# Nine token tiles transposed by DMA, a searched start-up order and VectorE exp from step 6 in a one-core attention and FFN kernel

## The chip, the cores and the metric

The kernel runs on one core of one Trainium2 chip. The metric is the device time of one execution in microseconds (us). Times of a kernel are medians of its runs; where two kernels are compared in several rounds, they ran in turn on the same chip. Runs marked "one look" below are single executions and have no interval. The traces are of one execution each. In the record the time of one and the same kernel goes with the mean clock granted to TensorE in that execution: the kernel before took 773.5 to 773.9 us where that was 0.996, and 778.6 to 778.8 us where it was 0.987 to 0.989. Differences of 1 to 2 us between two single traces are to be read with that in mind.

Engines are named as in the profile: PE is TensorE (matmul), PEld its weight loads, DVE is VectorE, ACT is ScalarE, POOL is GpSimd, SP is SyncE, and SPq is the queue from which SP issues DMA transfers.

## The reference

With S = 2048 tokens, D = 640, 32 heads of 20, one shared key head and one shared value head, and F = 1728:

```python
x  = A_x                                   # 1 x 2048 x 640, bf16
xn = layernorm(x)
q  = xn @ wq                               # 32 heads of 20
k  = xn @ wk ; v = xn @ wv                 # one head of 20 each
o  = softmax(q k^T / sqrt(20)) v           # 2048 x 2048 per head
return x + o @ wo + silu(xn @ w1) @ w2
```

## The kernel before

A list scheduler in Python places every instruction on its engine ahead of time, with a cost model of its own. On the chip the orders are fixed; only semaphores decide when an instruction starts. The scheduler also places filler matmuls on zeros, whose results nobody uses, where it expects TensorE to wait.

The main loop has 688 *steps*: 43 groups of three heads (for 512 queries) times 16 key tiles. A step is three score matmuls of 512 columns, the exp of the three blocks, and the products P·V of an earlier step. ScalarE takes three blocks of a step, or two when VectorE takes the third by integer arithmetic on the bits (a "VectorE exp"). VectorE exps need a second copy of the keys with an offset, `kT1`, which POOL writes.

Before the loop can run freely comes the start-up ("prologue"): 16 token tiles are normalised, transposed, and turned into keys (`k` jobs), values (`v` jobs) and queries (`q` jobs). `PRO` is the order of these jobs. They are interleaved with the first exp steps.

```python
NBLK = 34                                  # ring of exp results, blocks of 512
PRO = "t4 t5 t6 k2 t7 t8 k3 t9 t10 k4 t11 t12 k5 t13 t14 v0 k6 t15 k7 q1 v1 v2 v3"
...
self.xn = self.w2[:, 0:4, :]               # four slots for normalised tiles
...
def want_dve(self, t):                     # may step t give a block to VectorE?
    if self.pro_left or t % KT >= KT - NOD:    # not while prologue jobs are left
        return False
    back = ...                             # VectorE's backlog in the model
    return back < DVE_TH
...
def tr_job(n):                             # transpose of tile n: five matmuls into PSUM,
    ...                                    # then one copy out by VectorE or ScalarE
...
def k_job(j):
    ...                                    # VectorE copies the keys out of PSUM, then POOL:
    sc.new("pool", t_pool(256), lambda g: g.tensor_scalar(d1, dst, self.offk[:, :], 1.0, ALU.add,
                                                          ALU.mult), [("kT", j), ("offk",)], [("kT1", j)], ...)
```

Heads 0 to 7 get their queries from two early jobs. Head 8 (step 32 is the first that uses it) gets them from a later job, `q0_0`, which makes those of heads 8 to 14: five matmuls, one copy to SBUF by VectorE, and seven small copies from SBUF to SBUF, all issued by SP. They share one semaphore, so whoever needs one of the seven waits for all.

```python
def qd_job(self, c, m, step=-1):           # q0_0 is c = 0, m = 0: columns 160 to 287 of wq
    ...
    sem = sc.sem(f"q{c}_{m}")
    for h in range(lo // DH, -(-hi // DH)):    # one copy per head: seven of them
        ...
        ops.append(sc.dma("sp", lambda q, ...: q.dma_start(
            self.qT[r:r + z - a, h // 4, c % 2, :], self.qd[a - lo:z - lo, sl, :]), [("qd", sl)], ...,
            sem=sem, name="qdma"))
    for op in ops:
        op.inc_no = len(ops)               # a reader waits for the count of all
```

The softmax here doesn't subtract the row's maximum and nothing guards it: scores larger than these inputs give would overflow.

## Time and profile before

| | before |
|---|---|
| time, first three runs | 776.55 us (776.13 to 778.77) |
| span in the profile | 775.3 us |
| first exp on ScalarE | 18.22 us |
| exp of step 21 / step 32 / last (687) | 59.30 / 71.95 / 753.34 us |
| ScalarE busy, 18.2 to 58.6 us | 31.62 of 40.40 us |
| ScalarE busy, 80 to 748.9 us | 658.84 of 668.90 us |

The prediction shows the lines these come from. "Exp of step n" is the start of the exp that comes n-th on ScalarE, counted from 0 in the trace; as every step has exactly one, the same n is the same work in every kernel here. The difference of two such starts is called the *lead* of one kernel.

### The profile page before, as it was taken

To read this page: it belongs to the slowest core of one execution; us is meant where nothing else is said; L and a number is where in the kernel's file an instruction comes from. 1 tells how busy PE (TensorE), PEld (TensorE's weight loads), DVE (VectorE), ACT (ScalarE), POOL (GpSimd) and SP (SyncE) were. 2 spreads that over 40 slices of the span, in tenths; PEclk is the share of its full clock that TensorE was granted. 3 is DMA by queue.
4 is the path that set the end of the run, shared out by engine and by line. 5 is a ranking of instruction groups with operands and counts; after the bars stand their busy time and mean duration, and the time that the engine had idled before them with its cause. 6 is when DMAs were issued, how large, how long until landed. Compare 5 with 4: busy or idle time off the path is not lost. (4 is left out here: it accounts for less than half of the span.)

```text
span 775.3 us, 17568 instructions
## 1 busy us (share of the span) xinstructions
PE 742.5 (96%) x6934; PEld 245.8 (32%) x6934; DVE 681.3 (88%) x1350; ACT 725.8 (94%) x772; POOL 26.2 (3%) x73
## 2 busy tenths in 40 slices
PE   8888998999999999999999999999999999999997
PEld 4432222222233333322223333322223333222334
DVE  7547999999999898999999999899999799899985
ACT  6879999999999999999999999999999999999960
POOL 4800000000000000000000000000000000000000
PEclk9989999999999999999999999999999999999999
DMA  9130000000110000000001000000010000000100
GB/s 283 56 115 8 10 10 8 10 8 8 42 35 23 19 10 26 25 8 2 2 1 35 26 25 23 14 17 5 2 35 18 19 19 18 2 1 1 29 1 35
DMA packets 27062, 20.05 MB, mean 26 GB/s; under 512 B 14790, under 2 KB 26342, under 8 KB 26982
## 3 DMA queue, kind: packets, MB, share of 16 engines
q1 hardware_dynamic: 25670, 18.89, 8.5%
q8 instruction: 56, 0.92, 0.5%
q10 hardware_dynamic: 1312, 0.05, 0.1%
q14 instruction: 24, 0.20, 0.1%
HBM read 11.36 MB, written 2.62 MB: 18 GB/s over the span
## 5 line engine op out<-in xcount | busy, mean ns | idle before, releaser
L748 ACT ACTIVATE sbt<-psall 128x1024 bf16<-128x1024 f32 (+2 forms) x688 | 697.5, 1162 | 18.9 <-PE psall L730 14.4
L762 DVE TENSOR_SCALAR sbt<-psall 128x512 int16<-128x512 f32 x560 | 375.7, 685 | 42.9 <-PE psall L730 36.4
L730 PE MATMUL psall<-sbt 32*128 32x512 bf16 x2048 | 269.6, 385 | 18.9 <-ACT sbt L748 11.7
L808 PE MATMUL psall<-sbt 128*32 128x512 bf16 x3329 | 258.1, 384 | 0.8 <-DVE sbt L1400 0.4
L820 DVE TENSOR_SCALAR sbt<-sbt 128x1536 int16<-128x1536 int16 (+2 forms) x420 | 204.0, 507 | 4.4 <-PE psall L808 2.0
L730 PEld LDWEIGHTS psall<-sbt 32*128 32x128 bf16 x2048 | 69.5, 91 | 257.0 <-ACT sbt L748 117.8
L808 PEld LDWEIGHTS psall<-sbt 128*32 128x32 bf16 x3329 | 70.3, 95 | 113.1 <-issue 64.2
L986 PE MATMUL psall<-sbt 128*128 128x512 bf16 (+1 forms) x280 | 87.7, 388 | 1.8 <-DVE sbt L999 1.6
L1047 PE MATMUL psall<-sbt 128*128 128x320 bf16 x448 | 87.0, 302 | 1.1 <-DVE sbt L961 1.0
L1047 PEld LDWEIGHTS psall<-sbt 128*128 128x128 bf16 x448 | 35.1, 97 | 44.1 <-issue 32.7
L999 DVE SCALAR_TENSOR_TENSOR sbt<-sbt,psall 128x512 bf16<-128x512 bf16 (+1 forms) x56 | 38.2, 681 | 4.4 <-ACT sbt L994 4.0
L994 ACT ACTIVATE sbt<-psall 128x512 bf16<-128x512 f32 (+1 forms) x56 | 39.7, 708 | 0.0
L882 DVE CAST sbt<-psall 128x512 bf16<-128x512 f32 (+1 forms) x43 | 29.5, 685 | 5.0 <-PE psall L808 4.9
L986 PEld LDWEIGHTS psall<-sbt 128*128 128x128 bf16 (+1 forms) x280 | 19.3, 98 | 40.9 <-issue 28.2
L1052 PE MATMUL psall<-sbt 128*128 128x320 bf16 x160 | 30.4, 302 | 0.7 <-DVE sbt L1030 0.7
L667 PE MATMUL psall<-sbt 128*128 128x512 bf16 (+4 forms) x103 | 28.5, 408 | 1.9 <-POOL sbt L1199 1.4
L954 PE MATMUL psall<-sbt 128*128 128x512 bf16 (+1 forms) x95 | 28.0, 384 | 0.0
L654 PE MATMUL psall<-sbt 128*32 128x512 bf16 (+8 forms) x85 | 25.1, 353 | 0.0
L1070 DVE SCALAR_TENSOR_TENSOR sbt<-psall,sbt 128x320 bf16<-128x320 f32 x32 | 15.0, 485 | 4.1 <-PE psall L1052 3.1
L917 DVE TENSOR_TENSOR sbt<-psall,sbt 128x240 bf16<-128x240 f32 (+2 forms) x46 | 17.2, 379 | 0.2
L1052 PEld LDWEIGHTS psall<-sbt 128*128 128x128 bf16 x160 | 12.6, 97 | 13.1 <-issue 7.0
L1352 DVE COPY sbt<-psall 128x640 bf16<-128x640 bf16 x14 | 6.7, 489 | 10.3 <-PE psall L1341 10.1
(79 smaller groups left out, 179.6 us busy)
## 6 DMA issues: line engine op xcount, KB each, us to landing
sbt<-in_A_x_dram SPq DMA_DIRECT2D x32, 160.0 KB, 3.3
out_dram<-sbt SPq DMA_DIRECT2D x16, 160.0 KB, 1.8
sbt<-in_B_w_dram SPq DMA_DIRECT2D x5, 432.0 KB, 6.4
sbt<-sbt SPq DMA_DIRECT2D x105, 20.0 KB
sbt<-in_B_w_dram SPq DMA_DIRECT2D x13, 160.0 KB, 3.4
sbt<-in_A_wo_dram SPq DMA_DIRECT2D x5, 160.0 KB, 6.5
sbt<-in_A_wq_dram SPq DMA_DIRECT2D x5, 140.0 KB, 3.6
sbt<-sbt SPq DMA_TRANSPOSE x16, 2.6
```

What stands on the lines that cost most here:

```text
L667: return pe.matmul(self.bk(b, 0, n), self.zero[:, 0:P], self.zero[:, 0:n], start=True, stop=True)
L730: ins = pe.matmul(self.bk(par3 + j), self.kT[r:r + SLOT, kk, kt * P:(kt + 1) * P], self.qT[r:r + SLOT, h // 4, (x // H) % 2, :], start=Tru ...
L748: return a.activation(self.E[:, b0 * QW:(b0 + na) * QW], self.ps[:, par3 * BANK:(par3 + na) * BANK], AF.Exp, scale=ACT_SCALE)
L762: return v.tensor_scalar(self.Z[:, zs, zp * QW:(zp + 1) * QW], self.bk(bb), 0.0, ZMAX, ALU.max, ALU.min)
L808: return pe.matmul(self.bk(UBANK, 0, QW, q * SLOT, (q + 1) * SLOT), self.v[:, w, kt, :], x, start=start, stop=stop, tile_position=(0, q * ...
L820: sc.new("dve", t_dve_4x(w), lambda v, k=k: v.tensor_scalar(self.Y[:, zs, k, 0:n * QW], Z, float(PH[k + 1][0]), None, ALU.add), zk, [("Y", ...
L882: return v.tensor_copy(self.U[0:rows, up, :], self.bk(UBANK, 0, QW, 0, rows))
L986: return pe.matmul(self.bk(b, 0, QW, 0, rows), self.w1[:, k, fk * P:fk * P + rows], self.xnT[:, k, c * QW:(c + 1) * QW], start=(k == 0), s ...
L994: sc.new("act", t_act(QW), lambda a: a.activation(t, src, AF.Tanh, scale=0.5), [("B", b)], [("tb", tp)], prio=X_PRIO, name=f"th{c}_{fk}")
L999: sc.new("dve", t_dve_ps(QW), lambda v: v.scalar_tensor_tensor(out=self.hT[0:rows, fk, :], in0=t, scalar=1.0, in1=src, op0=ALU.add, op1=AL ...
L1047: return pe.matmul(self.bk(b, 0, 320), self.hT[0:rows, fk, i * P:(i + 1) * P], self.w2[0:rows, fk, e0:e0 + 320], start=(m == 0), stop=(m = ...
L1052: return pe.matmul(self.bk(b, 0, 320), self.oT[:, k, i * P:(i + 1) * P], self.wo[:, k, e0:e0 + 320], start=(m == 0), stop=(m == tot - 1))
```

## The change

The intent is a shorter start-up. Three parts can be told apart:

1. **Transposes.** Tiles 4 to 7 and 11 to 15 are transposed by DMA from SP's queue, and every normalised tile has its own place (`xa(n)`), where before there were four slots.
2. **Order.** A new order of the jobs, another division of the layer norm's statistics, square roots and norms among the engines, found by a search.
3. **VectorE exp from step 6.** `want_dve` no longer waits until the start-up jobs are done.

```diff
-PRO = "t4 t5 t6 k2 t7 t8 k3 t9 t10 k4 t11 t12 k5 t13 t14 v0 k6 t15 k7 q1 v1 v2 v3"
-ACT_STATS = (3, 6, 9, 12)
-NW_ENG = ("dve", "pool", "pool")
-NORM_ENG = ("pool",) * 4 + ("pool", "act") * 4
-BATCHES = ((0, 4), (4, 10), (10, 16))
+DT = (4, 5, 6, 7, 11, 12, 13, 14, 15)
+DVE_FROM = 6
+PRO = "v0 t8 t9 k2 t10 k3 k4 k5 q1 v1 k6 k7 v2 v3"
+ACT_STATS = (2, 4, 6, 8, 9, 12)
+NW_ENG = ("dve", "pool", "pool", "dve")
+NORM_ENG = ("dve", "act", "dve", "dve", "pool", "pool", "dve", "act", "dve", "pool", "act", "act")
+BATCHES = ((0, 4), (4, 8), (8, 12), (12, 16))
...
     def want_dve(self, t):
-        if self.pro_left or t % KT >= KT - NOD:
+        if t < DVE_FROM or t % KT >= KT - NOD:
             return False
...
-        self.xn = self.w2[:, 0:4, :]
+        def xa(n):
+            if n < 13:
+                return self.w2[:, n if n < 4 else n + 1, :]
+            return oflat[:, (n - 13) * D:(n - 12) * D]
...
+        for n in range(4, NT):
+            norm(n, NORM_ENG[n - 4], NORM_P, self.batch[n])
+            if n not in DT:
+                continue
+            op = sc.dma("sp", lambda q, n=n: q.dma_start_transpose(
+                self.xnT[:, :, n * P:(n + 1) * P], xa(n)), xnk(n), [("xnT", n)], D * P * 2,
+                sem=sem(f"xT{n}"), name="xTd")
```

(Cut: the issue of the loads of w1 and wo moves behind the transposes, the blank fills of qT move ahead of them, and the scheduler's model of DMA times is adapted.)

More of the change, by code (lines that the diff above doesn't have):

```diff
@@ L63 @@
 Q_EVERY = 2
-PRO = "t4 t5 t6 k2 t7 t8 k3 t9 t10 k4 t11 t12 k5 t13 t14 v0 k6 t15 k7 q1 v1 v2 v3"
-ACT_STATS = (3, 6, 9, 12)
-NW_ENG = ("dve", "pool", "pool")
-NORM_ENG = ("pool",) * 4 + ("pool", "act") * 4
-BATCHES = ((0, 4), (4, 10), (10, 16))
+DT_ISSUE = 1.28
+DT = (4, 5, 6, 7, 11, 12, 13, 14, 15)
+NORM_P = 0.05
+DVE_FROM = 6
[4 more added lines that the diff above has]
+BATCHES = ((0, 4), (4, 8), (8, 12), (12, 16))
 class Op:
@@ L178, in commit @@
         if op.dma:
+            if op.name in ("oTd", "xTd"):
+                self.dma_t = op.end
             self.dma_t = max(getattr(self, "dma_t", 0.0), op.end) + op.mode / 230e3
-            op.avail = max(op.end + (2.6 if op.name == "oTd" else 2.0), self.dma_t + 1.6)
+            op.avail = op.end + 1.6 if op.name in ("oTd", "xTd") else max(op.end + 2.0, self.dma_t + 1.6)
         else:
@@ L1016, in try_oT @@
                 sem=self.s_oT[i], name="oTd")
+            op.dur = DT_ISSUE
             op.inc_no = len(self.oT_made)
@@ L1176, in prologue @@
                            for c in range(DC)], ("wqd", 1), P * D * 2)
-        load_w("sp", "1", [lambda q, c=c: q.dma_start(self.w1[:, c, :], self.B_w1[c * P:(c + 1) * P, :])
-                           for c in range(DC)], ("w1",), P * F * 2)
-        load_w("sp", "o", [lambda q, c=c: q.dma_start(self.wo[:, c, :], self.A_wo[c * P:(c + 1) * P, :])
-                           for c in range(DC)], ("wo",), P * D * 2)
         w2p = []
@@ L1187, in load_w2 @@
         def load_w2():
-            load_w("sp", "2", w2p, ("w2",), P * D * 2, [("xn", i) for i in range(4)] + [("idf",)])
+            load_w("sp", "2", w2p, ("w2",), P * D * 2, [("xn", i) for i in range(14)] + [("idf",)])
         np_ = sc.new
@@ L1232, in prologue @@
                 [("idf",)], [("stk",)])
-        for c in range(DC):
-            pool(0.7, lambda g, c=c: g.tensor_scalar(self.wo[:, c, :], self.wo[:, c, :], 2.0, 1.0, ALU.mult, ALU.mult),
-                 [("wo",)], [("wo",)])
         def wkrep(a):
@@ L1277, in mvk, with xnk @@
             return [("mv", n) for n in range(a, b_)]
+        oflat = self.o[:, :, :, :].rearrange("p a b c -> p (a b c)")
+        def xa(n):
+            if n < 13:
+                return self.w2[:, n if n < 4 else n + 1, :]
+            return oflat[:, (n - 13) * D:(n - 12) * D]
+        def xnk(n):
+            return [("xn", n)] + (self.okeys if n >= 13 else [])
         def norm(n, eng, prio, ra):
-            xs = n % 4
             if eng == "act":
                 np_("act", t_act(D) + 0.186, lambda v: v.activation(
-                    self.xn[:, xs, :], self.xslot(n), AF.Identity, scale=self.rstd[:, n:n + 1],
-                    bias=self.nb[:, n:n + 1]), self.xkeys(n) + [("nb", n), ("rs", ra)], [("xn", xs), ("xnv", n)],
+                    xa(n), self.xslot(n), AF.Identity, scale=self.rstd[:, n:n + 1],
+                    bias=self.nb[:, n:n + 1]), self.xkeys(n) + [("nb", n), ("rs", ra)], [("xn", n)],
                     prio=prio, name=f"norm{n}")
@@ L1287, in norm @@
             np_(eng, 0.36 if eng == "dve" else 0.87, lambda v: v.tensor_scalar(
-                self.xn[:, xs, :], self.xslot(n), self.rstd[:, n:n + 1], self.nb[:, n:n + 1], ALU.mult, ALU.add),
-                self.xkeys(n) + [("nb", n), ("rs", ra)], [("xn", xs), ("xnv", n)], prio=prio, name=f"norm{n}")
+                xa(n), self.xslot(n), self.rstd[:, n:n + 1], self.nb[:, n:n + 1], ALU.mult, ALU.add),
+                self.xkeys(n) + [("nb", n), ("rs", ra)], [("xn", n)], prio=prio, name=f"norm{n}")
         def newton(a, b_, pr, eng):
@@ L1335, in prologue @@
                     norm(n, "dve", 0.05, a)
+        for n in range(4, NT):
[5 more added lines that the diff above has]
+                sem=sem(f"xT{n}"), name="xTd")
+            op.dur = DT_ISSUE
+            op.inc_no = 1
+        load_w("sp", "1", [lambda q, c=c: q.dma_start(self.w1[:, c, :], self.B_w1[c * P:(c + 1) * P, :])
+                           for c in range(DC)], ("w1",), P * F * 2)
+        load_w("sp", "o", [lambda q, c=c: q.dma_start(self.wo[:, c, :], self.A_wo[c * P:(c + 1) * P, :])
+                           for c in range(DC)], ("wo",), P * D * 2)
+        for c in range(DC):
+            pool(0.7, lambda g, c=c: g.tensor_scalar(self.wo[:, c, :], self.wo[:, c, :], 2.0, 1.0, ALU.mult, ALU.mult),
+                 [("wo",)], [("wo",)])
+        for par in range(2):
+            for ht in range(2 if par == 0 else 0, HT):
+                np_("dve", 0.31, lambda v, par=par, ht=ht: v.tensor_scalar(
+                    self.qT[:, ht, par, :], self.zero[:, 0:QW], self.offq[:, :], None, ALU.add),
+                    [("zero",), ("offq",)], [("qb", par, h) for h in range(4 * ht, 4 * ht + 4)],
+                    prio=6.0 + par, name="qz")
         def tr_job(n):
-            xs = n % 4
             mms = []
@@ L1340, in f @@
                 def f(pe, b, k=k):
-                    return pe.transpose(self.bk16(b)[:, k * P:(k + 1) * P], self.xn[:, xs, k * P:(k + 1) * P],
+                    return pe.transpose(self.bk16(b)[:, k * P:(k + 1) * P], xa(n)[:, k * P:(k + 1) * P],
                                         self.idb[:, :])
@@ L1347, in consume @@
                 dst = self.xnT[:, :, n * P:(n + 1) * P]
-                if n in (0, 2) or (n >= 4 and not self.started):
+                if n in (0, 2):
                     sc.new("act", t_act(D), lambda a: a.activation(dst, src, AF.Copy), [("B", b)], [("xnT", n)],
@@ L1353, in consume @@
                            prio=0.5 if n < 4 else 3.0, name=f"xT{n}")
-                if n == NT - 1:
+                if n == max(i for i in range(13) if i not in DT):
                     load_w2()
-                    for par in range(2):
-                        for ht in range(2 if par == 0 else 0, HT):
-                            np_("dve", 0.25, lambda v, par=par, ht=ht: v.tensor_scalar(
-                                self.qT[:, ht, par, :], self.zero[:, 0:QW], self.offq[:, :], None, ALU.add),
-                                [("zero",), ("offq",)], [("qb", par, h) for h in range(4 * ht, 4 * ht + 4)],
-                                prio=6.0 + par, name="qz")
-                if n + 4 < NT:
-                    m = n + 4
-                    norm(m, NORM_ENG[m - 4], 0.5, self.batch[m])
-            return Job(f"tr{n}", mms, [("xnv", n), ("xn", xs), ("idb",)], consume)
+            return Job(f"tr{n}", mms, xnk(n)[:1] + [("idb",)], consume)
         def k_job(j):
```

## The prediction

> **What bounds the kernel now.** I read the engine totals first, then the busy time by stretch, then the timeline of ScalarE over the first 70 us, and last the waits of that stretch. The totals of the page:
> ```profile
> PE 742.5 (96%) x6934; PEld 245.8 (32%) x6934; DVE 681.3 (88%) x1350; ACT 725.8 (94%) x772; POOL 26.2 (3%) x73
> ...
> L748 ACT ACTIVATE sbt<-psall 128x1024 bf16<-128x1024 f32 (+2 forms) x688 | 697.5, 1162 | 18.9 <-PE psall L730 14.4
> L762 DVE TENSOR_SCALAR sbt<-psall 128x512 int16<-128x512 f32 x560 | 375.7, 685 | 42.9 <-PE psall L730 36.4
> ```
> TensorE's 96% contains filler matmuls, so it is no proof. The 688 exps of ScalarE (one per step: three 512-wide score blocks, or two when VectorE takes the third) fill 697.5 of 775.3 us. Whether that binds everywhere shows in the busy time by stretch (columns: window, its length, busy us of each engine with its count of instructions, granted TensorE clock, DMA share, GB/s):
> ```profile
> 0.00:18.20 18.20, 16.09 (x84) 7.54 (x84) 12.87 (x48) 10.73 (x23) 8.28 (x35) 1.00 0.89 274
> 18.20:58.60 40.40, 35.39 (x316) 15.22 (x314) 20.33 (x64) 31.62 (x26) 17.91 (x39) 0.92 0.29 95
> 58.60:80.00 21.40, 18.68 (x175) 5.94 (x178) 16.82 (x34) 20.13 (x21) 0.00 (x0) 1.00 0.03 7
> 80.00:748.90 668.90, 651.72 (x6215) 205.96 (x6207) 614.24 (x1167) 658.84 (x697) 0.00 (x0) 1.00 0.06 16
> 748.90:776.00 27.10, 20.64 (x160) 11.11 (x156) 17.02 (x39) 4.46 (x7) 0.00 (x0) 0.92 0.07 25
> ```
> From 80 to 748.9 us ScalarE is busy 658.84 of 668.90 us: that loop is bound by exp. In the start-up it is not: between the first exp (18.22 us) and 58.6 us ScalarE idles 40.40 - 31.62 = 8.8 us, and VectorE works only 20.33 of 40.40 us. ScalarE's timeline (start, us taken, operation, count, idle before) says where:
> ```profile
> 18.22 5.48 ACT L748 ACTIVATE sbt<-psall 128x1536 bf16<-128x1536 f32 x4 [0.81 <-PE psall L730]
> ...
> 27.91 0.92 ACT L1282 ACTIVATE sbt<-sbt 128x640 bf16<-128x640 bf16 x1 [2.99 <-PE psall L1341]
> 28.73 2.77 ACT L748 ACTIVATE sbt<-psall 128x1536 bf16<-128x1536 f32 x2
> ...
> 46.11 1.45 ACT L748 ACTIVATE sbt<-psall 128x1536 bf16<-128x1536 f32 x1 [1.08 <-PE psall L730]
> 51.31 16.90 ACT L748 ACTIVATE sbt<-psall 128x1536 bf16<-128x1536 f32 x15 [3.75 <-PE psall L808]
> ```
> Two big holes. At 24.9 us a norm needs the slot that the transpose of an earlier tile still holds (only four slots), and TensorE waits for the square root of tiles 4 to 9 on POOL. At 47.6 us the 34-block ring of exp results is full, and the products P·V that would free it wait for v jobs placed last in the order. All of the first 21 exps are three blocks wide; the first VectorE exp begins at 58.62 us, the first two-block one on ScalarE at 59.30 us.
>
> **What the Trainium skill says.** "Perfetto Trace Analysis", Optimization Strategy, says that a kernel can have several regimes, and to look for the gaps of the engine that should be full; that is the reading above, and the trace agrees (78% busy in the start-up, 98.5% in the loop). "DMA: Bandwidth & Descriptors", DMA Transpose, allows a transpose only from the SP or ACT queue, for 2-byte types, into SBUF; and two streams of them must not overlap. Here all come from SP, so one stream. The kernel before already has 16 of them: issue 1.23 us, landing 2.6 us in the median (2.4 to 4.1). "TensorE: Matmul & The Clock Gate", Part 4, says that a transpose on TensorE ends in PSUM and needs a copy out: here 489 ns on VectorE each. Part 1 there says that the clock halves after an idle window; this trace has 0.76 granted from 40 to 50 us, where three scores take 0.61 us, not 0.39.
>
> **The change part by part.** I compared the built order of instructions of both kernels; it holds no times. I price it with durations of the trace.
>
> *1. Transposes.* Nine of 16 tiles leave TensorE: 45 matmuls fewer (80 to 35), some 9 x 0.45 = 4 us there, and nine copies out fewer, 9 x 0.49 = 4.4 us of VectorE. In return SP issues nine DMA transposes, 9 x 1.23 = 11 us of a queue that is idle then (its weight loads of w1 and wo move behind it). Each normalised tile now has its own place, so no norm waits for a slot. None of this is on the exp chain as such; it removes the 2.99 us hole and gives TensorE and VectorE room.
>
> *2. Way to the first exp.* Filler before the first transposes shrinks from 39 to 35.4 matmuls of 0.29 us, so they start about 1 us sooner (12.75 to about 11.9 us). The copies of tiles 0 and 2 on ScalarE stand back to back, where a 0.73 us statistic lay between. Against it: three more halves of statistics (0.86 us start to start) before the first exp, partly in the 1.91 us hole before the first copy; and VectorE's first blank fill of qT waits for an offset that POOL had at 6.51 us, so the first root does not start earlier (8.63 us before). Estimate: first exp at 17.4 us, 0.8 earlier.
>
> *3. ScalarE work up to step 21.* Of the first 21 exps, 12 shrink from three to two blocks (in all: 572 VectorE exps for 560; counted step by step the lead of 12 arises in the first 21 steps and stays at 12 to the end). A back-to-back three-block exp takes 1.335 us ((31.39 - 28.73)/2), a two-block one 0.97 (533.5/550). So 12 x 0.365 = 4.4 us less. One half of a statistic comes after the first exp: +0.86. Four norms and one weight copy stay.
> Before: 21 x 1.335 + 4 x 0.83 + 0.5 = 31.9 us of work, and 8.8 of holes, give 40.7; measured 59.30 - 18.22 = 41.1. After: 9 x 1.335 + 12 x 0.97 + 3.3 + 0.5 + 0.86 = 28.3 us of work.
>
> *4. Holes left.* The norm of tile 5 stands on ScalarE directly after the first exp and needs a root chain on POOL of 12 instructions, 3.4 us (16.40 to 19.79 before); I put its end at 18.8, as the first exp ends: no hole, or 1 us. The keys of steps 4 and 5 need tiles 4 and 5 by about 23 us (two transposes landed), used at 27.6: fine. Transposes of tiles 11 to 15 go out in order, the last after the norm of tile 15 on ScalarE (about 27 us): landing by 32, its keys are wanted at step 14, near 38. The first P·V now stands before step 14's scores, just when the ring is full: about 1 us. Steps 12 to 20 then carry four v jobs' rest, q1 and all of P·V with VectorE's pieces; before, the same region had holes of 0.36 to 1.08 us per step, so I leave 2 us. In sum 3.8 us for 8.8.
>
> *Sum:* step 21 begins at 17.4 + 28.3 + 3.8 = 49.5 instead of 59.3 us: -9.8. Behind it the steps hold the same work in the same widths, so the shift is kept. I take 0.3 off for a start-up that presses more on VectorE. 776.55 - 9.5 = **767.0 us**, -1.2%.
>
> **Rivals.**
> *VectorE becomes the bound of the start-up.* Twelve exps (0.6 us start to start) and their phase copies (two of 0.5 us per three blocks) put 7.2 + 4 us more on it, the nine norms it now does part of some more, minus 4.4 of copies. It had 20 us free in this stretch, now shorter by 10. It would be near 85% full between 28 and 50 us, like the loop's 92%; waits of 1 to 4 us more are possible: 768 to 771. For it: the v evacuations stand between exps. Against: the order gives a three-block exp whenever VectorE lags.
> *The transposes come late.* SP works in order, so one late norm holds all behind. If each landing were 4 us, tile 15 lands near 34 us, still before 38: hidden, 767. Only if they slowed beside other traffic to 8 us would steps 4 or 12 wait: 771. The traffic of w1 now comes after them, which speaks against.
> *The loop gives it back.* If the loop were bound by something with fixed times, the shift would vanish: 776. ScalarE's 98.5% there and the same counts behind step 21 speak against it. A shift can change which waits fall together in the loop, +-1 us.
> *Almost no holes left.* 0.5 us of holes and a first exp at 16.6: 763.
>
> **Range and chances.** The work of ScalarE sets a floor: no holes at all would give 767.0 - 3.8 = 763.2, and an earlier first exp 762.5. Faster by over 2% needs 761.0, below that floor; I leave 4% for a loop that runs better than now. The high end, 771.5, is the VectorE rival in full with a slow first exp. Slower by over 2% would take 792 us, a new stall of 25 us: 1%.
>
> **What would show it.** In the changed profile: first exp near 17.4 us; the 22nd exp near 49.5 us; ScalarE idle by 3 to 5 us between them; the transposes landing in 2.4 to 3 us and the last before 33 us; no hole of 3 us at all; 572 VectorE exps, the first near 30 us; the loop from 80 us on at 98 to 99% of ScalarE; the tail from the last exp unchanged (some 21 us). Wrong it would be if a key or v block came late (a hole in front of an exp, released by a matmul that waited for a transpose), if the first exp came at 18 us or later, or if the loop's ScalarE share fell.

## The result, and the profile after

The changed kernel took **772.85 us** (772.82 to 774.07, four runs) against 777.66 us (776.13 to 778.82) of the kernel before in the same rounds. The ratio is 0.9943, with a 95% interval of 0.9919 to 0.9967. The change gains 0.6%, which is within 2%, as the prediction had said was most likely; but the time lies above the forecast range of 762.5 to 771.5 us. About half of the forecast gain of 9.5 us came: 4.8 us by the medians, 4.4 us by the ratio.

The engine totals and the two exp lines of the page after:

```profile
PE 737.9 (96%) x6892; PEld 241.6 (31%) x6892; DVE 690.1 (90%) x1375; ACT 724.5 (94%) x780; POOL 23.5 (3%) x68
...
L753 ACT ACTIVATE sbt<-psall 128x1024 bf16<-128x1024 f32 (+2 forms) x688 | 692.4, 1146 | 20.5 <-PE psall L735 18.5
L767 DVE TENSOR_SCALAR sbt<-psall 128x512 int16<-128x512 f32 x572 | 383.8, 685 | 49.7 <-PE psall L735 41.0
```

ScalarE's exps fell by 5.1 us (697.5 to 692.4), yet the idle time before them did not fall: 18.9 before, 20.5 now. The busy time by stretch after, with the columns as in the prediction:

```profile
0.00:18.20 18.20, 15.82 (x102) 7.92 (x102) 13.44 (x55) 14.08 (x30) 9.27 (x39) 1.00 0.67 192
18.20:58.60 40.40, 32.95 (x294) 12.37 (x292) 33.70 (x94) 35.25 (x36) 14.25 (x30) 0.92 0.55 168
58.60:80.00 21.40, 18.57 (x169) 4.98 (x169) 14.30 (x27) 16.15 (x17) 0.00 (x0) 0.84 0.03 7
80.00:748.90 668.90, 654.48 (x6211) 206.66 (x6209) 616.14 (x1174) 658.06 (x700) 0.00 (x0) 1.00 0.06 16
```

The second line is the success: ScalarE is busy 35.25 us of the 40.40, where it was 31.62. The fourth, the long loop, is as it was (658.06 for 658.84). The third is the news: from 58.6 to 80 us ScalarE works 16.15 of 21.40 us, where before it worked 20.13. And the granted TensorE clock there is 0.84, where it was 1.00. ScalarE's timeline of the changed kernel (start, us taken, operation, count of merged instructions, idle time before) shows the holes:

```profile
17.25 1.43 ACT L753 ACTIVATE sbt<-psall 128x1536 bf16<-128x1536 f32 x1
...
25.83 1.73 ACT L1289 ACTIVATE sbt<-sbt 128x640 bf16<-128x640 bf16 x2 [0.74 <-DVE sbt L1326]
...
32.32 5.12 ACT L753 ACTIVATE sbt<-psall 128x1024 bf16<-128x1024 f32 x5 [0.18 <-PE psall L735]
38.60 1.02 ACT L753 ACTIVATE sbt<-psall 128x1024 bf16<-128x1024 f32 x1 [1.16 <-PE psall L735]
40.93 1.02 ACT L753 ACTIVATE sbt<-psall 128x1024 bf16<-128x1024 f32 x1 [1.30 <-PE psall L813]
42.78 1.02 ACT L753 ACTIVATE sbt<-psall 128x1024 bf16<-128x1024 f32 x1 [0.82 <-PE psall L735]
44.29 16.95 ACT L753 ACTIVATE sbt<-psall 128x1536 bf16<-128x1536 f32 x16 [0.49 <-PE psall L735]
61.58 1.45 ACT L753 ACTIVATE sbt<-psall 128x1536 bf16<-128x1536 f32 x1 [0.33 <-PE psall L735]
65.71 1.02 ACT L753 ACTIVATE sbt<-psall 128x1024 bf16<-128x1024 f32 x1 [2.68 <-PE psall L735]
67.66 1.02 ACT L753 ACTIVATE sbt<-psall 128x1024 bf16<-128x1024 f32 x1 [0.93 <-PE psall L735]
69.16 1.02 ACT L753 ACTIVATE sbt<-psall 128x1024 bf16<-128x1024 f32 x1 [0.48 <-PE psall L735]
```

The holes of 2.99 and 3.75 us of the kernel before are gone. There are several of about 1 us between 38 and 44 us, and one of 2.68 us at 65.71, where there was a smaller one before. All engines together show what it waits for. Here is the kernel before, at the same step (65.71 after is 71.95 before):

```profile
64.17 0.68 DVE L961 TENSOR_SCALAR sbt<-psall 128x512 bf16<-128x512 f32 x1
...
64.88 5.33 SPq L969 DMA_DIRECT2D sbt<-sbt  x7
...
71.52 0.39 PE L730 MATMUL psall<-sbt 32*128 32x512 bf16 x3 [1.51 <-DMA sbt<-sbt]
...
71.95 1.02 ACT L748 ACTIVATE sbt<-psall 128x1024 bf16<-128x1024 f32 x1 [0.99 <-PE psall L730]
```

And the changed kernel:

```profile
57.75 0.63 DVE L966 TENSOR_SCALAR sbt<-psall 128x512 bf16<-128x512 f32 x1
...
58.40 5.34 SPq L974 DMA_DIRECT2D sbt<-sbt  x7
...
65.05 0.61 PE L735 MATMUL psall<-sbt 32*128 32x512 bf16 x3 [2.82 <-DMA sbt<-sbt]
...
67.00 0.61 PE L735 MATMUL psall<-sbt 32*128 32x512 bf16 x3
```

This is job q0_0: VectorE's copy, then seven copies on SP that take 5.34 us to issue (0.76 each), then the scores of step 32. In both kernels the scores start 1.31 us after the last issue ends (64.88 + 5.33 + 1.31 = 71.52; 58.40 + 5.34 + 1.31 = 65.05). So this step is not set by ScalarE: it comes 6.47 us earlier because the issue came 6.48 us earlier, while ScalarE was ahead by 7.9 us one step before. After the wait of 2.82 us, three scores take 0.61 us instead of 0.39 until 71.7 us: TensorE's clock is halved.

The lead by step tells what that costs (starts in us, counted from the traces; the last line is `before` minus `after`; the three experiments of the table are described below):

| step | 0 | 21 | 31 | 32 | 40 | 96 | 687 |
|---|---|---|---|---|---|---|---|
| before | 18.22 | 59.30 | 69.48 | 71.95 | 81.38 | 141.20 | 753.34 |
| after | 17.25 | 50.59 | 61.58 | 65.71 | 77.23 | 136.69 | 748.80 |
| q_two_queues | 17.35 | 50.69 | 61.68 | 63.33 | 72.26 | 131.80 | 743.33 |
| hole_filled | 17.30 | 50.31 | 61.16 | 65.15 | 74.08 | 133.47 | 744.79 |
| dve_late | 17.22 | 50.92 | 61.01 | 62.34 | 72.05 | 129.66 | 741.46 |
| lead of after | 0.97 | 8.72 | 7.90 | 6.24 | 4.15 | 4.51 | 4.54 |

The lead is 8.72 us at step 21, where 9.8 were forecast. It shrinks from 7.90 to 4.15 us between steps 31 and 40, and from there to the last exp it hardly moves. Behind step 21, most of the loss lies at one place; the 0.8 us between steps 21 and 31 are taken up at the end.

### The profile page after: what moved, and what is told of

Same layout as the page of the kernel before. It is cut to its first block, busy times and chain, and to the rows that moved or that the text cites. A ratio compares the mean times of both kernels' runs of the same rounds, so it can differ in the third digit from the quotient of the medians. Undisturbed runs are those within 1.5% of the kernel's fastest.

```text
span 770.8 us, 17543 instructions
## 1 busy us (share of the span) xinstructions
PE 737.9 (96%) x6892; PEld 241.6 (31%) x6892; DVE 690.1 (90%) x1375; ACT 724.5 (94%) x780; POOL 23.5 (3%) x68
## 5 line engine op out<-in xcount | busy, mean ns | idle before, releaser
L753 ACT ACTIVATE sbt<-psall 128x1024 bf16<-128x1024 f32 (+2 forms) x688 | 692.4, 1146 | 20.5 <-PE psall L735 18.5
L767 DVE TENSOR_SCALAR sbt<-psall 128x512 int16<-128x512 f32 x572 | 383.8, 685 | 49.7 <-PE psall L735 41.0
L813 PE MATMUL psall<-sbt 128*32 128x512 bf16 x3355 | 262.8, 387 | 0.2
L825 DVE TENSOR_SCALAR sbt<-sbt 128x1536 int16<-128x1536 int16 (+2 forms) x430 | 207.7, 505 | 4.4 <-PE psall L813 2.0
L991 PE MATMUL psall<-sbt 128*128 128x512 bf16 (+1 forms) x280 | 88.9, 390 | 2.1 <-DVE sbt L1004 1.6
L887 DVE CAST sbt<-psall 128x512 bf16<-128x512 f32 x43 | 29.5, 685 | 4.9 <-PE psall L813 4.8
L959 PE MATMUL psall<-sbt 128*128 128x512 bf16 (+1 forms) x95 | 28.6, 385 | 0.0
L672 PE MATMUL psall<-sbt 128*128 128x512 bf16 (+3 forms) x91 | 25.3, 406 | 1.7 <-POOL sbt L1201 1.4
L659 PE MATMUL psall<-sbt 128*32 128x512 bf16 (+9 forms) x74 | 21.5, 346 | 0.0
L966 DVE TENSOR_SCALAR sbt<-psall 128x512 bf16<-128x512 f32 (+1 forms) x19 | 12.9, 679 | 0.0
```

The costliest lines, as they stand in the source:

```text
L753: return a.activation(self.E[:, b0 * QW:(b0 + na) * QW], self.ps[:, par3 * BANK:(par3 + na) * BANK], AF.Exp, scale=ACT_SCALE)
L767: return v.tensor_scalar(self.Z[:, zs, zp * QW:(zp + 1) * QW], self.bk(bb), 0.0, ZMAX, ALU.max, ALU.min)
L813: return pe.matmul(self.bk(UBANK, 0, QW, q * SLOT, (q + 1) * SLOT), self.v[:, w, kt, :], x, start=start, stop=stop, tile_position=(0, q * ...
L825: sc.new("dve", t_dve_4x(w), lambda v, k=k: v.tensor_scalar(self.Y[:, zs, k, 0:n * QW], Z, float(PH[k + 1][0]), None, ALU.add), zk, [("Y", ...
L887: return v.tensor_copy(self.U[0:rows, up, :], self.bk(UBANK, 0, QW, 0, rows))
L959: return pe.matmul(self.bk(b, 0, QW, 0, rows), self.wq[:, k, lo:hi], self.xnT[:, k, c * QW:(c + 1) * QW], start=(k == 0), stop=(k == DC - 1))
```

## The experiments

Theory A: the start-up gain is real, and the wait for q0_0's copies, with the lowered clock behind it, takes almost 4 us of it. Rival B: something in the changed order (more work on VectorE, other widths) loses it there anyway, and the wait for the copies is only what the profile names last. Separately, the first 21 steps: which part makes their gain, and do the twelve VectorE exps in them pay?

### q_two_queues: three of the seven copies from POOL's queue

```diff
-                ops.append(sc.dma("sp", ...
+                side = c == 0 and m == 0 and len(ops) % 2
+                ops.append(sc.dma("pool" if side else "sp", ...
```

The three copies have a semaphore of their own. The orders of the compute engines are identical to the changed kernel's.

> The changed kernel with one thing moved: three of the seven small copies that bring the queries of heads 8 to 14 to their place are issued from POOL's queue, four from SP's. All instructions on TensorE, VectorE and ScalarE keep their order. Theory A (the gain of the start-up is given back at step 32, whose scores wait for the last of these copies, issued one after another at 0.76 us each): the last issue comes 2.3 us sooner, the wait of 2.82 us before step 32 shrinks below 1 us, the granted clock from 60 to 80 us rises from 0.83 to near 1.00, and the time falls from 772.9 to about 769.5. Rival B (the give-back is a backlog of VectorE and TensorE that a start-up with 12 more VectorE exps leaves behind): the wait moves elsewhere, 772 to 773. Rival C (POOL's copies take longer to start): no better, 772 to 773.

Measured: **767.14 us** (766.15 to 767.24), ratio to before 0.9879 [0.9863, 0.9895]. The timeline around step 32:

```profile
58.51 3.09 SPq L976 DMA_DIRECT2D sbt<-sbt  x4
...
58.80 1.80 POOL L976 DMA_DIRECT2D sbt<-sbt  x3 [10.60 <-DVE sbt L922]
...
62.90 0.39 PE L735 MATMUL psall<-sbt 32*128 32x512 bf16 x3 [0.56 <-DMA sbt<-sbt]
...
63.33 3.03 ACT L753 ACTIVATE sbt<-psall 128x1024 bf16<-128x1024 f32 x3 [0.20 <-PE psall L735]
```

Four issues on SP end at 61.60, and the scores start 1.30 us later, at 62.90. The wait is 0.56 us, the scores take 0.39 us, so the clock was not lowered, and the lead stays at 9 to 10 us to the end. Nothing but the issue of three small transfers was moved, and 5.7 us came back by the medians, 5.0 by the ratios (0.9943 - 0.9879, times 776). Theory A holds, B falls: with the same orders the shift is kept. The 769.5 us expected were too high: more came back than Theory A had counted on.

### q_mid: job q0_0 earlier in the order

```diff
-PRO = "v0 t8 t9 k2 t10 k3 k4 k5 q1 v1 k6 k7 v2 v3"
+PRO = "v0 t8 t9 k2 t10 k3 k4 k5 q1 v1 k6 k7 v2 d0 v3"     # d0 is q0_0
```

> The changed kernel with the matmul job for the queries of heads 8 to 14 placed before the last job of the values (v3) instead of behind it, so its copies start some 5 us sooner. Theory A: no wait for a copy before step 32, clock near 1.00 from 60 to 80 us, the lead over the kernel before at step 40 about 7.5 us instead of 4.15, and 769 to 770 us. Rival B (backlog): the lead at step 40 is still 4 to 5 us, 772 to 773.

Measured: **770.32 us** (769.67 to 770.82), ratio 0.9921 [0.9902, 0.9940]. The copies are issued at 53.8 us and the wait before step 32 is gone; the clock from 60 to 80 us is 1.00. But the last v job is pushed back (its last matmul stands behind the scores of 26 steps, for 23), and a new hole of 2.01 us stands before the exp at 59.23 us. The lead is 4.7 us at step 31 and 7.2 at step 40. So moving the job cures this wait too, but brings only a third of the benefit (0.9921, where the split brought 0.9879 from 0.9943), because it makes another.

### hole_filled: ten dummy matmuls in the wait

Ten matmuls on zeros are put ahead of step 32's scores; nothing else moves. This leaves the wait and takes away only what it does to the clock.

```diff
+        if t == 32 and self.forced < 10 and self.u_open:
+            self.forced += 1
+            ...   # one matmul of zeros, 512 columns, into the open P·V bank
```

> The changed kernel with ten idle matmuls of 512 columns on zeros put in front of the last products before step 32; nothing else moves. They lie inside the 2.82 us wait. If the lowered clock after that wait (0.61 us for three scores from 65 to 71 us) is what costs the second part of the give-back: step 32 begins as before (65.1 us), the clock stays 1.00, the lead at step 40 is near 6 us instead of 4.15, and the time about 771. If the clock is not the cause: 772.9, same lead. If the matmuls delay the step: slower, 773 to 774.

Measured: **770.34 us** (768.75 to 771.63), ratio 0.9922 [0.9901, 0.9942]. The busy time from 60 to 80 us, first of the changed kernel and then of this one:

```profile
60.00:80.00 20.00, 17.17 (x157) 4.58 (x154) 12.93 (x24) 14.75 (x16) 0.00 (x0) 0.83 0.03 7
```

```profile
60.00:80.00 20.00, 19.30 (x195) 6.04 (x187) 15.66 (x30) 17.17 (x20) 0.00 (x0) 1.00 0.03 7
```

The exp of step 32 still waits (hole of 2.54 us), but the clock is 1.00 instead of 0.83 and ScalarE works 2.4 us more. The lead at step 40 is 7.30 us instead of 4.15, a difference of 3.15 us between the two traces. Of this, 0.42 us was there at step 31 already, ahead of the dummies (8.32 against 7.90), so 2.7 us are left for the lowered clock. The traced execution was the fastest of this kernel's four; over all runs the ratios (0.9922 against 0.9943) are worth 1.6 us, and their intervals overlap. The clock's share of the loss is therefore some 1.6 to 2.7 us, not known more closely.

### dve_late: the third part of the change undone

VectorE exps start only when the prologue jobs are done, as in the kernel before; parts 1 and 2 stay.

```diff
-        if t < DVE_FROM or t % KT >= KT - NOD:
+        if self.pro_left or t % KT >= KT - NOD:
```

> The changed kernel with the third part undone: VectorE takes its first exp only when the start-up jobs are all done, as in the kernel before. Theory A: with three-block exps for 12 more steps, step 32 is reached about 4.4 us later, near 69 us, when the queries would be there: no wait for a copy before it; so the time is about the same, 772 to 774.5. If the VectorE exps had given most of the measured gain, it would be near 777.

Measured: **765.57 us** (764.26 to 767.35), ratio 0.9863 [0.9842, 0.9884]. The expectation failed: without its third part the change is better by 6 to 7 us (0.9943 - 0.9863, times 776, is 6.2; the medians differ by 7.3). ScalarE's timeline and its busy time from the first exp to the exp of step 21:

```profile
28.50 9.51 ACT L753 ACTIVATE sbt<-psall 128x1536 bf16<-128x1536 f32 x7 [0.53 <-PE psall L735]
38.36 1.45 ACT L753 ACTIVATE sbt<-psall 128x1536 bf16<-128x1536 f32 x1 [0.36 <-PE psall L735]
40.21 17.76 ACT L753 ACTIVATE sbt<-psall 128x1536 bf16<-128x1536 f32 x16 [0.40 <-PE psall L735]
...
58.28 5.18 ACT L753 ACTIVATE sbt<-psall 128x1024 bf16<-128x1024 f32 x5
```

```profile
17.22:50.92 33.70, 28.40 (x258) 11.54 (x259) 21.21 (x72) 31.66 (x30) 14.06 (x33) 0.95 0.65 201
```

The same stretch of the changed kernel, which ends with its own step 21:

```profile
17.25:50.59 33.34, 27.21 (x238) 10.54 (x235) 27.95 (x82) 28.19 (x30) 14.95 (x33) 0.90 0.66 203
```

This pair is the second finding. By step 21 the changed kernel has 12 VectorE exps, this one 3. The nine more take 3.47 us of work off ScalarE (28.19 for 31.66 us), but step 21 comes only 0.33 us earlier. The rest turned into holes (5.15 us for 2.04). ScalarE was the bound of this stretch only as long as it was full; freed of 3.5 us it waits for scores and for P·V.

One rival is not excluded. The traces show that TensorE ran at half clock (granted 0.50) from 37.35 to 44.18 us in the changed kernel, just where its holes lie, but only from 35.99 to 39.40 us in dve_late, and not at all before step 21 in late_two_queues, the next run, which has the orders of dve_late (step 21 at 49.86 us there, 1.06 us sooner). Three scores took 0.61 us in that stretch, for 0.39 after it. So a part of the extra holes may be the lowered clock and not the VectorE exps as such, and the 0.33 us is smaller than what two executions of one order differ by. No run separates the two.

The extra exps also push jobs back. Counted in the instruction orders, q0_0's first matmul stands behind the scores of 25 steps in the kernel before, of 27 in the changed one, and of 21 here. Its copies are issued from 54.11 us here, for 58.40, and step 32 meets no hole at all:

```profile
54.11 5.65 SPq L974 DMA_DIRECT2D sbt<-sbt  x7
```

### late_two_queues: dve_late and the split copies together

> VectorE exps only after the start-up jobs (as in the run dve_late, 765.6 us) and the copies for heads 8 to 14 split over SP's and POOL's queues; all compute engines keep the order of dve_late. Theory A2 (in dve_late the queries come in time, as ScalarE has no hole in front of step 32): the split gives nothing, 765 to 766 us. If a part of the wait for the queries is left there: 763 to 764.

Measured: **764.93 us** (764.81 to 765.41), ratio 0.9852 [0.9817, 0.9888]. With the early issue there is nothing left to win from the split: 0.6 us, inside the spread. Read the other way, with the copies split in both, the third part of the change costs 2.2 us (767.14 against 764.93, the intervals just overlap) instead of 6 to 7: by this difference, some two thirds of its cost came by way of q0_0. The rest isn't lost in the start-up alone: with only 5 VectorE exps fewer in all (567 for 572), but 9 fewer by step 21, this schedule has four more of them afterwards, worth 4 x 0.365 = 1.5 us by the prediction's figure. This is the fastest version, 10.4 us below the median of the kernel before in the same rounds (775.30). Not tried was a semaphore of its own for head 8's copy, the only one of the seven that step 32 needs.

### k1_dve: the second key copy by VectorE

In the changed kernel TensorE's scores wait for POOL's offset copies (1.73 us before the scores at 37.89 us). Is POOL's copy the cause of the holes at 38 to 43 us, or is VectorE's load? In this experiment VectorE writes the copy straight from PSUM.

```diff
-                sc.new("pool", t_pool(256), lambda g: g.tensor_scalar(d1, dst, self.offk[:, :], 1.0, ALU.add, ...
+                sc.new("dve", t_dve_ps(256), lambda v: v.tensor_scalar(d1, src, self.offk[:, :], None, ALU.add), ...
```

> The changed kernel with the second copy of the keys (the one with the offset for VectorE's exps) written by VectorE from PSUM, not by POOL from the first copy. Theory D1 (the holes of 1.2, 1.3 and 0.8 us in front of the exps of steps 12 to 14 start with TensorE's wait of 1.73 us for POOL's copy before step 12, which also lowers the clock): that wait goes, and the lead over the kernel before at step 21 grows from 8.7 to 10 us or more. Rival D2 (the load of VectorE itself makes the holes): with 6 x 0.43 us more on VectorE the lead stays below 9 us. The wait for the queries before step 32 stays in both, so the time stays near 772.

Measured: 773.76 us. The wait for POOL is gone, and nothing is gained: a hole of 2.33 us now stands at 41.20, released by the P·V products, and the lead at step 21 is 8.26 us, for 8.72. D1's lead of 10 us did not come, and the forecast of D2 (below 9 us) holds. But the run doesn't settle which of them is right. The scores that waited 1.73 us for POOL now wait 0.91 us for VectorE's copy; two VectorE exps fewer fall before step 21 (10 for 12); and the clock, which D1 had in its account, was halved as before, from 37.60 to 44.43 us. What the holes would be at full clock stays untested.

### dve12 and dve12_two_queues: VectorE exps from step 12

```diff
-DVE_FROM = 6
+DVE_FROM = 12
```

dve12_two_queues adds the split copies.

> The changed kernel with VectorE exps from step 12 instead of 6: between the changed kernel (772.9, 12 such exps by step 21) and dve_late (765.6, 3 by step 21). If each early VectorE exp costs more than it saves: in between, 767 to 771. If only the ones of steps 6 to 11 hurt, as they fall on the stretch where the keys' second copies are made: near 766.

> The two findings together: VectorE exps from step 12, and the copies for heads 8 to 14 split over two queues; compute engines in the order of dve12. In dve12 step 21 came at 49.1 us, the earliest of all, and 3.2 us were then lost waiting for the queries before step 32, with a lowered clock behind it. If that wait is the only thing that gives the gain back: step 32 near 61.5 us instead of 64.3, clock 1.00 from 60 to 80 us, and 764 to 766 us, the range of late_two_queues (764.9). If the early VectorE exps cost something besides: 767 or more.

dve12: 770.80 us, inside the first branch of its expectation (767 to 771) and not near the 766 of the second. Step 21 comes at 49.08 us (lead 10.2), the earliest in any trace. That doesn't show that the VectorE exps of steps 12 to 20 pay: dve12_two_queues, whose compute engines have the same order, reached step 21 at 51.31 us, and the order of dve_late reached it at 50.92 us in one trace and at 49.86 in the other. Which of the early exps cost, and which pay, is not shown. In dve12 q0_0's copies are late again (TensorE waits 3.16 us before step 32), and the lead falls to 6.6 us at step 40.

dve12_two_queues missed the 764 to 766 us that were expected if the wait alone gave the gain back: **770.72 us** (769.09 to 771.54), ratio 0.9914 [0.9893, 0.9934], no better than the one look at dve12, and in the branch "767 or more". The wait before step 32 did shrink to 0.9 us. But with the same order of the compute engines the clock was lowered earlier. The busy time from 40 to 50 us, dve12 and then dve12_two_queues:

```profile
40.00:50.00 10.00, 8.06 (x89) 3.29 (x90) 8.32 (x20) 10.00 (x12) 4.12 (x6) 1.00 0.84 301
```

```profile
40.00:50.00 10.00, 8.95 (x68) 2.58 (x67) 5.97 (x15) 8.55 (x9) 4.12 (x6) 0.66 0.84 301
```

The clock granted is 0.66 where it was 1.00, and step 21 comes 2.2 us later. Why the clock fell, long before the split copies, stays open. It was no exception: of the four executions the mean granted clock was 0.987 in three, the traced one among them, and 0.991 in the fourth (late_two_queues: 0.993 to 0.997). One look at dve12 (0.991) can't say what is usual there. late_two_queues stays the best version.

### before_dve6: the third part alone on the kernel before

```diff
-        if self.pro_left or t % KT >= KT - NOD:
+        if t < 6 or t % KT >= KT - NOD:
```

> The kernel before with VectorE exps from step 6 on; the third part of the change alone. If these exps only trade ScalarE's work for waits (theory D): the time stays within 3 us of the kernel before, and ScalarE's idle time between the first exp and step 21 grows by what its work shrinks. If they are worth their 4.4 us: 772.

Measured, one look: 781.49 us, with 775.30 us as the median of the kernel before in those rounds. Step 21 comes at 59.70 us (0.4 later), and the last exp 4.3 us later. TensorE's scores wait 4.7 us for POOL's offset keys, and ScalarE has holes of 2.53, 5.01 and 2.34 us in front of its exps. So neither branch of the expectation came true: not within 3 us, and not 772. A part of the loss is again the wait for q0_0's copies, issued from 69.57 us: TensorE waits 3.78 us for them before step 32, and the lead goes from -2.08 us at step 31 to -4.70 at step 32. In this one execution, the third part alone costs (781.49 us lies above the highest of all runs of the kernel before, 778.82).

### late_pe_tr and late_pe_tr2: all tiles transposed by TensorE

dve_late with `DT = ()`, so part 1 undone except for the separate places, and the transposes back in the order.

> As dve_late, but all sixteen tiles are transposed by TensorE, in the changed kernel's own slots and with its statistics; the first part of the change undone. It adds 45 matmuls (4 us of TensorE) and nine copies (4.4 us of VectorE) to the first 45 us, where VectorE in dve_late is busy under half of the time after 30 us. If the transposes by DMA carry the gain, step 21 comes 3 us or more later than in dve_late (50.9 us) and the time is 769 or more. If the own slots and the order of jobs carry it, 765.5 to 767.5.

late_pe_tr: 777.35 us (776.50 to 778.93), ratio 1.0013 [0.9981, 1.0046]. It says little: the job q1 stood ahead of the transposes of tiles 12 to 15 and waited for a weight copy on a full ScalarE, which made a hole of 9.12 us. The second try puts the transposes and key jobs ahead of q1 and the weight copy early.

> late_pe_tr again, mended: there, a query job that waits for a weight copy on a full ScalarE stood ahead of the transposes of tiles 12 to 15 and made a hole of 9.1 us, which says nothing of the transposes. Here all transposes by TensorE and the key jobs come before it, and the weight copy runs early. If the transposes by DMA matter only through TensorE's and VectorE's 4 us each (which dve_late had free): step 21 at 51 to 53 us, 766 to 768 us. If they matter because every job in that stretch must pass through the one or two PSUM banks left beside the scores: step 21 at 55 us or later, and 770 us or more.

late_pe_tr2: **779.20 us** (778.40 to 779.53), ratio 1.0038 [1.0010, 1.0067], 13.6 us more than dve_late; step 21 at 59.89 us, for 50.92. ScalarE's timeline there:

```profile
42.91 2.79 ACT L753 ACTIVATE sbt<-psall 128x1536 bf16<-128x1536 f32 x2 [1.31 <-PE psall L735]
46.91 1.45 ACT L753 ACTIVATE sbt<-psall 128x1536 bf16<-128x1536 f32 x1 [1.21 <-PE psall L735]
51.88 10.91 ACT L753 ACTIVATE sbt<-psall 128x1536 bf16<-128x1536 f32 x9 [3.53 <-PE psall L813]
```

The old hole in front of P·V (3.75 us in the kernel before) is back with 3.53 us. In these orders the gain of the start-up hangs on the DMA transposes; more room for the normalised tiles and the other order do not give it alone. The order was searched for DMA transposes and not for this case, so 13.6 us is an upper mark for what they are worth. That the PSUM banks are the reason, as the second branch of the expectation has it, is not shown, though the numbers lie on its side. The other way round, DMA transposes in the old order, was not tried.

### before_two_queues: the split copies on the kernel before

> The kernel before with the copies for heads 8 to 14 split over two queues. There TensorE waited 1.51 us for them before step 32 and ScalarE 0.99: the theory that this floor became binding only with the faster start-up says 0.5 to 1.5 us faster than the kernel before, lead at step 40 near 1.3 us, and no more.

Measured, one look: 773.15 us (before 775.23 in those rounds). Around step 32 the lead grows by 1.5 us (3.7 to 5.2), the size of the wait of 1.51 us that it takes away. The lead of 3.7 us ahead of it is no effect of the edit: the compute orders are identical up to there. In this execution the clock from 40 to 50 us was 1.00, in the trace of the kernel before 0.76. One order of the compute engines varies by this much in its start-up; the kernel before ranged from 773.5 to 778.8 us.

## Why the prediction was wrong, point by point

**What held.** The first exp: 17.4 us forecast, 17.25 measured. ScalarE's work to step 21: 28.3 forecast, 28.19 measured. The transposes: nine issued between 19.24 and 32.1 us, 1.28 us each, landed after 2.4 to 3.2 us (the last at 33.52 us, 0.5 later than forecast), and no wait of TensorE before step 21 was ended by one of them. A key did come late in another way, through POOL's second copy: the scores of step 12 waited 1.73 us for it. 572 VectorE exps, the first at 30.91 us. The loop at 98.4% of ScalarE (658.06 of 668.90), so the rival of a loop that gives it back falls. The tail is unchanged.

**The step that failed.** "Behind it the steps hold the same work in the same widths, so the shift is kept." The shift was not kept: 7.90 us at step 31 became 4.15 at step 40. As to the work, the sentence is nearly right (the changed kernel is ahead by 12 VectorE exps at step 21, by 10 at step 31, and by 12 again at step 96 and at the end). But step 32 does not wait for work. It waits for a chain with a length of its own (VectorE's copy 0.63 us, issue 5.34, landing 1.3), which starts when q0_0's matmuls are done. Before, this chain was almost hidden (1.51 us of TensorE, 0.99 of ScalarE). With ScalarE 8 us further ahead and the chain only 6.5, it became the bound for one step: 1.66 us of lead lost at step 32, and 2.09 more up to step 40, with the clock lowered (hole_filled, which keeps the wait but not the lowered clock, loses 1.02 us in all from step 31 to 40). q_two_queues shows it by taking away nothing but the wait and what follows from it. The forecast had read a transfer list for the transposes alone; the wait of 1.51 us stood in the trace before, and the comparison of the orders, read before the forecast, has q0_0's first matmul behind the scores of 27 steps instead of 25.

**The term that was mis-sized.** "So 12 x 0.365 = 4.4 us less" was counted in full, with holes put at 3.8 us. The holes were 5.15 us. dve_late undoes nine of the twelve exps, 3.3 us of the 4.4 by the same figure, and step 21 comes 0.33 us later, because its holes are 2.04 us. In these two traces nine tenths of what the nine saved turned into waiting. The rival "VectorE becomes the bound of the start-up" had the right place and size (1 to 4 us) for this stretch, but its mechanism is not shown: VectorE was busy 17.01 of the 22 us from 28 to 50 us, 77% where the rival had 85%. The waits show a mixture of VectorE, POOL and P·V, with TensorE at half clock for 6.83 us, rather than one engine. Neither the sum nor a rival had it that these exps would also delay the issue of q0_0's copies by 4 us (54.11 to 58.40).

**The sum.** Forecast 9.8 at step 21; too few holes counted, less a first exp 0.15 us better: -1.1 (8.72). Steps 21 to 31: -0.8; the changed kernel has 7 VectorE exps there, the kernel before 9, so ScalarE works 10.66 us for 10.18, and it has a hole of 0.33 us. The prediction's "stays at 12 to the end" is off by two exps for these steps. The wait and the clock: -3.75. Later: +0.4. Together 4.5 us in the traces, and 4.8 by the medians.

## What to carry to other kernels

When a start-up is made shorter, list every transfer that later steps need for the first time, with the time of its issue and the slack it had; a chain of serial small issues keeps its length and becomes the wait. Taking work off the bound engine pays only as far as its inputs come earlier, so read the hole in front of it before counting the work saved. Undo each part of a bundled change alone: here the third part cost more than half of what the other two had won. And look at the granted clock before two single traces are compared: one order reached step 21 at 49.1 us in one execution and at 51.3 us in another.

## What the Trainium skill lacked or had wrong

- "DMA: Bandwidth & Descriptors", section "Issuing engines are not separate DMA queues", says that issuing from several engines saves only sequencer time, "which is usually small relative to the DMA itself". For a chain of small copies it was the larger part here: seven copies of 20 KB at most took 5.34 us to issue from SP, and then 1.31 us from the end of the last issue to the use. Splitting the issue between SP and POOL (1.80 us for three there) was worth 5 to 5.7 us of the whole time, the lowered clock behind the wait included. "Perfetto Trace Analysis", section "DMA Optimizations", has the remedy, balancing across engines when the issue is the bottleneck; that agrees.
- Neither of these pages has the time that SP takes here to issue one plain copy within SBUF (0.76 us) or one transpose of a 128 x 640 bf16 tile within SBUF (1.28 us, landing after 2.5 us in the median). The first is what a chain of small copies has to be priced with.
- "TensorE: Matmul & The Clock Gate", Part 1, puts the fall to half clock after an idle window of about 3.4 us. Here less was enough. The changed kernel ran at half clock from 64.66 us on, after TensorE had been idle for 2.43 of the 3.41 us before (the stretches at half clock last 3.41 or 6.83 us in these traces, up to the last exp), and from 37.35 us on after 1.57 of 3.41; dve_late did from 35.99 us on after 0.83 of 3.41. But the kernel before had 1.51 of 3.41 us idle from 68.75 us and kept its full clock, so these traces give no new limit; as one for planning, 3.4 us of idle time is too generous here. The page also says that the window runs freely, which fits: kernels with the same order up to there fell to half clock at 37.35, 37.65 and 36.36 us (after, q_two_queues, hole_filled).
